# Retention and a gated feed-forward in one kernel: the hand-written order of the lead-in, and of units 4 to 7, rewritten

## The chip, the cores and the metric

The kernel runs on one core of one Trainium2 chip. The metric is the device time of one launch in microseconds. The median of four runs of the kernel before is 298.68 us (298.44 to 298.91).

## The reference

Two layers follow each other. The first is a decayed linear attention (retention) over 8 batches, 8 heads, 576 positions and a head size of 64. The second is a feed-forward of width 2048 over the resulting 4608 tokens of width 512.

```python
scores = scale * np.matmul(q, k.transpose(0, 1, 3, 2))
gamma  = 1.0 - 2.0 ** (-5.0 - np.arange(H))
Dmat   = np.where(rel >= 0, gamma[:, None, None] ** rel[None], 0.0)   # rel = row - column
x = np.matmul(scores * Dmat, v)      # then (B, S, H * D) -> tokens x 512
h = x @ w_in
out = (h * sigmoid(1.702 * h)) @ w_out
```

Because the decay is a power of the distance, the part of the sum that lies in earlier blocks of 64 positions can be carried in a state of 64 x 64 per head; only the block on the diagonal needs scores and a mask.

## The kernel before

**Units and chunks.** The 4608 tokens are cut into 36 units of 128 rows, four units to a chunk, so nine chunks. A unit has two blocks of 64 rows. For each unit the kernel computes x transposed (in xT), and for each chunk the two products of the feed-forward: "up" (x with w_in, 16 steps f of 128 columns, and the Gelu into gT) and "down" (gT with w_out, four units r by four steps s of four matmuls each, then a copy to osb and a store).

**The steps of a unit, with their lines.**
- `load_kq` (L214), `load_v` (L227): DMAs issued by GpSimd (POOL); k and q are cast to bf16 on the way. Twelve slots each. `load_win` (L252) and `load_wout` (L259) bring the weights, each in four parts; they stand in the same queue.
- `transpose_pe` (L344) transposes k or q on TensorE (PE) into a PSUM bank; `transpose_copy` copies it to kqT, on ScalarE (ACT, L354) or VectorE (DVE, L357). `transposes` does both for a unit. From unit 8 on `dma_transpose` (L371) on SyncE's queue (SP) takes their place.
- `scale_v` (L336, DVE) multiplies v with the inverse decay, giving vp.
- `scores` (L477, PE, banks C and D) and `scores_out` (L486, DVE), which applies the mask and writes pm.
- The state. For units 0 to 3, `state_half` (L383 on PE, bank K, and L393 on ACT) accumulates in PSUM and casts after each block. Later, `state_both` (L406, banks K and E) makes both blocks' updates, `state_sum` (L419, L421, DVE) adds them to the running sum in stm, and `state_cast` (L430, ACT) casts the sums of some units to kv.
- `inter` (L461, PE, banks X and Y) multiplies q with the state, `values` (L499, PE) adds masked scores times vp in two halves, and `x_out` (L514) or `x_out_pair` (L524) multiplies with the decay factors gq on DVE and writes xT.

`block1(u)` is inter, values, second state half, values and x_out for one unit. `block(j)` is the same for the pair of units 2j and 2j+1, with the next pair's `ahead` (scores and state_both) between the two halves of values, and the next pair's `ahead_out` (masks, sums, cast) after the x_outs.

**What sets the order.** Nothing but the order in which the program calls these functions: each engine gets its instructions as a list, in that order, and waits on semaphores that are worked out from the names of tiles and banks read and written (`op`, class Program). No scheduler moves anything. An engine therefore stands still when the instruction at its head waits, whatever is behind it. The order is written out by hand in `lead_in` (units 0 to 3 and the up steps of chunk 0, then its down steps with a table `work` that hangs steps of units 4 to 7 on (r, s)), and in `steady` for chunks 1 to 8. `warm` (L649) issues matmuls whose result nobody reads.

**Banks.** A and B take the results of up and down in turn; a bank is free again when ACT has read it (Gelu at L541 or L555, copy to osb at L572). Up is done at full width by `up` (L536) or in groups of two or four steps over one or two units by `up_group` (L550).

**Where the change lies.** In chunk 0 the down steps are called in the order (0,0), (1,0), (0,1), (1,1), (0,2), (1,2), (0,3), (1,3), then (2,0) to (2,3) and (3,0) to (3,3). Before the change, units 4 and 5 are transposed after (0,3) and (1,3), their scores and states come at (2,0), units 6 and 7 are transposed after (2,1) and (2,3), and block(2), with the scores and states of units 6 and 7 inside, stands after (3,0). block(3) stands behind the fourth of chunk 1's sixteen up groups. In chunk 1's down steps, ahead(4) stands after (0,0), block(4) after (1,0), block(5) after (2,2).

Of the kernel before, what the change touches and what calls it, by code (L numbers as in the profile page):

```python
# [13 lines left out]
P = 128  # L14
# [144 lines left out]
def bass_retnet_parallel__then__act_gelu_quick_kernel(  # L159
# [10 lines left out]
    with es:  # L170
# [340 lines left out]
        def x_out(u, slot, hh):  # L511
            ch, j = divmod(u, 4)
            ty = unit_info(u)[2]
            op("dve", lambda e: e.tensor_tensor(  # L514
                xT[ch % 2][:, slice(hh, 4, 2), P * j : P * j + P], xbank(hh, slot),
                gq[:, ty, slice(hh, 4, 2), :], ALU.mult),
               reads=[XB[hh]] + [f"gq{a}_{ty}" for a in range(4)],
               writes=[xkey(u, hh)])
# [67 lines left out]
            scores_out(u, 1, 0)  # L586
            scores_out(u, 1, 1)

        def block1(u):
            started.clear()  # L590
            inter(u, u % 2)
            o = values(u, u % 2, 0)
            if unit_info(u)[1] < 2:
                state_half(u, 1)
            values(u, u % 2, 1, [o])
            x_out(u, u % 2, 0)
            x_out(u, u % 2, 1)

        def ahead(j):
            if 2 * j < NU:  # L600
# [5 lines left out]
        def ahead_out(j, cast=True):  # L606
            if 2 * j >= NU:
                return
            scores_out(2 * j, 2, 0)
            scores_out(2 * j, 2, 1)  # L610
            for u in (2 * j, 2 * j + 1):
                for a in range(2):
                    state_sum(u, a)
            if cast:
                state_cast(2 * j, 2 * j + 2)

# [27 lines left out]
            o = down_out(c, r, b, **kw)  # L644
            last_store[o.dma] = o

        def warm(n):
            for i in range(n):
                op("pe", lambda e: e.matmul(  # L649
                    bank["A"].ap(), gT[1][:, 0, 0:P], gT[1][:, 0, :], skip_group_check=True),  # L650
                   reads=["warm"], writes=["A"])

        def gelu_table():
            op("act", lambda e: e.activation(gT[1][:, 1, 0:4], gT[1][:, 0, 0:4], AF.Gelu_apprx_sigmoid),
# [2 lines left out]
        def lead_in():  # L657
            load_kq0(0)
            load_kq0(1)
            iota_small()  # L660
            iota_large()
            load_v(0)
            load(1)
            load_win(0)
            load(2)
            load_win(1)
            load(3)
            load_win(2)
# [12 lines left out]
            g_powers()  # L681
            gelu_table()
            cast_kq0(0, "dve")
            cast_kq0(1, "dve")
            transpose_pe(0, 0, "E")
            transpose_copy(0, 0, "E", "dve")
            warm(1)
            transpose_pe(0, 1, "B")
            transpose_copy(0, 1, "B", "act")
            warm(4)  # L690
            scores(0)
            scale_v(0)
            gq_next(1)
            scores_out(0, 1, 0)
            scores_out(0, 1, 1)
            state_half(0, 0)
            warm(2)
            transpose_pe(1, 0, "E")
            transpose_copy(1, 0, "E", "act")
            warm(1)  # L700
            transpose_pe(1, 1, "B")
            transpose_copy(1, 1, "B", "act")
            gq_next(2)
            block1(0)
            scale_v(1)
            warm(2)
            scores(1)
            warm(3)
            state_half(1, 0)
            scores_out(1, 1, 0)  # L710
            scores_out(1, 1, 1)
            warm(3)
            block1(1)
            warm(4)
            up_group(0, 0, 2, 0, 2, "A")
            transpose_pe(2, 0, "E")
            transpose_copy(2, 0, "E", "dve")
            up_group(0, 2, 2, 0, 2, "B")
            transpose_pe(2, 1, "E")
            transpose_copy(2, 1, "E", "act")  # L720
            warm(2)
            scale_v(2)
            scores(2)
            state_half(2, 0)
            gq_next(3)
            scores_out(2, 1, 0)
            scores_out(2, 1, 1)
            warm(2)
            up_group(0, 4, 2, 0, 2, "A")
            block1(2)  # L730
            up_group(0, 6, 2, 0, 2, "B")
            transpose_pe(3, 0, "E")
            transpose_copy(3, 0, "E", "dve")
            up_group(0, 0, 4, 2, 3, "A")
            transpose_pe(3, 1, "E")
            transpose_copy(3, 1, "E", "act")
            scale_v(3)
            up_group(0, 4, 4, 2, 3, "B")
            state_half(3, 0)
            scores(3)  # L740
            scores_out(3, 1, 0)
            scores_out(3, 1, 1)
            up_group(0, 8, 2, 0, 2, "A")
            block1(3)
            up_group(0, 10, 2, 0, 2, "B")
            up_group(0, 8, 2, 2, 4, "A")
            up_group(0, 10, 2, 2, 4, "B")
            up_group(0, 0, 4, 3, 4, "A")
            up_group(0, 4, 4, 3, 4, "B")
            gq_next(4)  # L750
            gq_next(5)
            for f in range(12, NF):
                up(0, f)
            def after8():
                ahead(2)
                scores_out(4, 2, 0)
                scores_out(4, 2, 1)

            def after9():
                transposes(6, "B", "B")  # L760
                for u in (4, 5):
                    state_sum(u, 0)
                    state_sum(u, 1)
                scale_v(6)
                scale_v(7)
                state_cast(4, 6)

            work = {
                (0, 3): lambda: (scale_v(4), transposes(4, "E", "E")),
                (1, 3): lambda: (scale_v(5), transposes(5, "C", "C")),  # L770
                (2, 0): after8,
                (2, 1): after9,
                (2, 3): lambda: transposes(7, "C", "C"),
                (3, 0): lambda: block(2, cast=False),
            }
            for r, s in [(i % 2, i // 2) for i in range(8)] + [(i // 4, i % 4) for i in range(8, NF)]:
                down(0, r, s, "AB"[r % 2])
                if (r, s) in work:
                    work[r, s]()
                if s == 3:  # L780
                    finish_unit(0, r, "AB"[r % 2])

        def steady():
            for c in range(1, NCH):
# [10 lines left out]
                if c == 1:  # L795
                    for i in range(16):
                        f0, lo = 2 * (i % 8), 2 * (i // 8)
                        up_group(1, f0, 2, lo, lo + 2, "AB"[i % 2])
                        if i == 1:
                            state_cast(6, 8)  # L800
                        if i == 3:
                            block(3, lambda: None)
                            scale_v(8)
                            scale_v(9)
                        if i == 8:
                            scale_v(10)
                            scale_v(11)
                else:
                    for f in range(NF):
                        up(c, f)  # L810
                        if f % 4 == 0:
                            m = 4 * c + 6 + f // 4
                            if m < NU:
                                scale_v(m)
# [11 lines left out]
                for r in range(4):  # L826
                    for s in range(4):
                        down(c, r, s, "AB"[r % 2])
                        if c == 1 and r == 1 and s == 0:
                            scale_v(12)  # L830
                            scale_v(13)
                        if c == 1 and (r, s) == (0, 0):
                            ahead(4)
                            ahead_out(4)
                        if (r, s) in (((1, 0), (2, 2)) if c == 1 else ((0, 0), (2, 0))):
                            j = 2 * c + 2 + r // 2
                            if 2 * j < NU:
                                block(j, cast=j != 5)
                    finish_unit(c, r, "AB"[r % 2])
                    if c == 1 and r == 3:  # L840
                        state_cast(12, 14)

        lead_in()
        steady()
# [60 lines left out]
```

## Time and profile before

| | us |
|---|---|
| median of four runs | 298.68 |
| the profiled execution's own time | 298.68 |
| its span (first to last instruction) | 296.9 |
| PE busy | 286.4 |
| ACT busy | 135.0 |
| POOL busy | 108.1 |
| DVE busy | 98.7 |

The times are those of one profiled execution. The granted TensorE clock is full over the whole span. A few per cent of the matmul records are missing; a hole of 0.2 us with no reason in a row of matmuls is such a record. A busy share of PE is an upper bound, since matmuls are pipelined and their ends are modelled; start times are what to compare. The chain of waits is read from the last instruction back: at each step it goes to what released the instruction, or to the one before it on its engine. PEld is the weight load of a matmul. "issue" in the chain is time in which an engine waited for nothing that the profile shows.

Landmarks of the PE's start times in the timeline: first up group 13.88, chunk 0's first down step 33.59, chunk 1's up steps 52.80, its down steps 68.00, chunk 2's up steps 85.02, its down steps 99.40.

### The profile page before, as it was taken

Reading aid. Unit: us, or ns where it says so; the run is one execution under the profiler, and the core shown is the slowest. Engines: PE = TensorE matmul, PEld = TensorE weight load, DVE = VectorE, ACT = ScalarE, POOL = GpSimd, SP = SyncE. Lnnn points to the kernel's source line nnn. Section 1 sums busy time; section 2 is a strip of 40 time slices with the busy share of each in tenths; the row PEclk is TensorE's granted clock in tenths of the full one; section 3 lists DMA queues with packets and bytes.
Section 4 is the critical chain, followed back from the end, with each engine's and each line's share of the span. In section 5 each row is a group of like instructions: output and inputs, shape, how many; then the busy total and the mean of one; then the engine's idle time right before and its main releaser. Section 6 shows DMA issues by size and latency. Waiting matters only on the chain.

```text
span 296.9 us, 7882 instructions
## 1 busy us (share of the span) xinstructions
PE 286.4 (96%) x3551; PEld 141.8 (48%) x3583; DVE 98.7 (33%) x198; ACT 135.0 (45%) x236; POOL 108.1 (36%) x137
## 2 busy tenths in 40 slices
PE   8989998999999999999999999999999999999996
PEld 2568455785533454345434543454344434443344
DVE  6555037424661345024701480038005700410000
ACT  8346444573246324642464237523652275216611
POOL 9999488000870760291029401930080000000000
PEclk9999999999999999999999999999999999999999
DMA  9999999979999995599269926991994050110021
GB/s 156 185 208 206 202 221 251 248 127 162 129 233 169 116 202 173 121 167 185 80 138 132 208 69 162 149 201 45 177 92 92 36 144 0 38 73 35 0 73 71
DMA packets 117234, 40.63 MB, mean 137 GB/s; under 512 B 106064, under 2 KB 110416, under 8 KB 117200
## 3 DMA queue, kind: packets, MB, share of 16 engines
q0 software_dynamic: 80160, 22.81, 67.0%
q1 hardware_dynamic: 37040, 17.31, 23.6%
q8 instruction: 28, 0.46, 0.6%
q14 instruction: 6, 0.05, 0.1%
HBM read 36.70 MB, written 9.44 MB: 155 GB/s over the span
## 4 chain that ended last, share of the span: by engine, by line
PE 87%; POOL 4%; DMA 4%; ACT 2%; issue 2%; DVE 1%; POOLq 0%; DVEq 0%
PE psA L562 20%; PE psB L562 20%; PE psA L536 17%; PE psB L536 16%; DMA w_in_sb<-in_moe_w_in_dram 4%; PE psA L550 3%; PE psB L550 3%; POOL kqn L214 2%; PE psX L461 2%; POOL vn L227 1%; PE psC L477 1%; POOL w_in_sb L252 1%; PE psX L499 1%; PE psY L499 1%; PE psK L406 1%
## 5 line engine op out<-in xcount | busy, mean ns | idle before, releaser
L214 POOL DMA_DIRECT2D kqn<-in_k_dram x39 | 35.5, 919 | 111.6 <-DMA kqT<-kqn 108.9
L562 PE MATMUL psA<-w_out_sb,gT 128*128 128x512 bf16 (+1 forms) x287 | 66.6, 373 | 2.8 <-issue 2.4
L562 PE MATMUL psB<-w_out_sb,gT 128*128 128x512 bf16 (+1 forms) x285 | 63.7, 373 | 1.0 <-issue 1.0
L536 PE MATMUL psA<-xT,w_in_sb 128*128 128x512 bf16 x231 | 59.3, 379 | 0.4 <-ACT gT L541 0.4
L536 PE MATMUL psB<-xT,w_in_sb 128*128 128x512 bf16 x225 | 59.2, 379 | 0.4
L524 DVE TENSOR_TENSOR xT<-psX,gq 128x512 bf16<-128x512 f32 x16 | 11.1, 691 | 119.7 <-PE psX L499 119.7
L430 ACT ACTIVATE kv<-stm 128x1024 bf16<-128x1024 f32 (+1 forms) x16 | 15.2, 949 | 68.6 <-DVE stm L421 68.6
L562 PEld LDWEIGHTS psB<-w_out_sb,gT 128*128 128x128 bf16 x288 | 27.8, 98 | 32.6 <-issue 1.2
L562 PEld LDWEIGHTS psA<-w_out_sb,gT 128*128 128x128 bf16 x304 | 27.7, 98 | 31.8 <-ACT gT L541 2.5
L541 ACT ACTIVATE gT<-psA 128x512 bf16<-128x512 f32 x58 | 34.6, 597 | 15.7 <-PE psA L536 15.7
L541 ACT ACTIVATE gT<-psB 128x512 bf16<-128x512 f32 x58 | 34.6, 597 | 15.2 <-PE psB L536 15.2
L227 POOL DMA_DIRECT2D vn<-in_v_dram x40 | 37.4, 941 | 2.3 <-issue 2.2
L214 POOL DMA_DIRECT2D kqn<-in_q_dram x39 | 35.7, 926 | 0.5 <-issue 0.5
L536 PEld LDWEIGHTS psA<-xT,w_in_sb 128*128 128x128 bf16 x232 | 18.5, 97 | 32.0 <-ACT gT L541 16.4
L536 PEld LDWEIGHTS psB<-xT,w_in_sb 128*128 128x128 bf16 x232 | 18.1, 97 | 31.9 <-ACT gT L541 15.5
L336 DVE TENSOR_TENSOR vp<-vn,vfac 128x512 bf16<-128x512 f32 x36 | 23.2, 684 | 23.0 <-DMA vn<-in_v_dram 23.0
L572 ACT ACTIVATE osb<-psB 128x512 f32<-128x512 f32 (+1 forms) x18 | 10.6, 587 | 21.6 <-PE psB L562 21.4
L486 DVE TENSOR_TENSOR pm<-psC,mask 128x512 bf16<-128x512 f32 (+1 forms) x20 | 12.6, 629 | 10.7 <-PE psD L477 10.7
L572 ACT ACTIVATE osb<-psA 128x512 f32<-128x512 f32 x18 | 10.6, 587 | 11.4 <-PE psA L562 11.4
L550 PE MATMUL psA<-xT,w_in_sb 128*128 128x256 bf16 (+1 forms) x128 | 14.6, 259 | 0.4 <-DMA w_in_sb<-in_moe_w_in_dram 0.3
L550 PE MATMUL psB<-xT,w_in_sb 128*128 128x256 bf16 (+1 forms) x128 | 14.6, 259 | 0.0
L486 DVE TENSOR_TENSOR pm<-psD,mask 128x512 bf16<-128x512 f32 (+1 forms) x20 | 12.5, 626 | 0.0
(67 smaller groups left out, 257.1 us busy)
## 6 DMA issues: line engine op xcount, KB each, us to landing
vn<-in_v_dram POOLq DMA_DIRECT2D x32, 256.0 KB, 5.4
out_dram<-osb SPq DMA_DIRECT2D x31, 256.0 KB, 2.2
kqn<-in_k_dram POOLq DMA_DIRECT2D x31, 128.0 KB, 5.0
kqn<-in_q_dram POOLq DMA_DIRECT2D x31, 128.0 KB, 5.3
w_in_sb<-in_moe_w_in_dram POOLq DMA_DIRECT2D x8, 256.0 KB, 8.8
w_out_sb<-in_moe_w_out_dram POOLq DMA_DIRECT2D x4, 512.0 KB, 16.6
out_dram<-osb SPq DMA_DIRECT2D x10, 128.0 KB, 2.6
vn<-in_v_dram POOLq DMA_DIRECT2D x8, 128.0 KB, 5.5
```

What stands on the lines that cost most here:

```text
L214: e.dma_start(kqn[sl][p0 : p0 + n, which, :, :], src[b, :, s0 : s0 + n, :].rearrange("h p d -> p h d"),)
L227: e.dma_start(vn[sl][p0 : p0 + n, :, :], v[b, :, s0 : s0 + n, :].rearrange("h p d -> p h d"))
L336: op(eng, lambda e: e.tensor_tensor(vp[u % NVP].ap(), vn[sl].ap(), vfac[:, ty, :, None].to_broadcast([P, H, DH]), ALU.mult), reads=[f"vn{s ...
L430: op("act", lambda e: e.activation(kv[:, i0 % NKV : i0 % NKV + n, :, :], stm[:, i0 % 8 : i0 % 8 + n, :, :], AF.Copy), reads=[f"stm{(i0 + i ...
L461: op("pe", lambda e, g=g, pb=pb, hh=hh, hp=hp, s=s, a=a, i=prev[a]: e.matmul(xbank(hh, slot)[64 * pb : 64 * pb + 64, g, 64 * a : 64 * a + 64],
L486: op("dve", lambda e: e.tensor_tensor(pm[(u0 // 2) % 2][hh][:, c0:c1].rearrange("p (a i) -> p a i", i=64), ps32(SB[hh])[:, c0:c1].rearrang ...
L524: op("dve", lambda e: e.tensor_tensor(xT[ch % 2][:, slice(hh, 4, 2), P * jj : P * jj + 2 * P].rearrange("p g (u t) -> p u g t", u=2), ps32 ...
L536: op("pe", lambda e, a=a: e.matmul(bank[b][:, n0:n1], w_in_sb[:, a, P * f : P * f + P], xT[c % 2][:, a, n0:n1], start=(a == 0), stop=(a == ...
L541: op("act", lambda e: e.activation(gT[c % 2][:, f, n0:n1], bank[b][:, n0:n1], AF.Gelu_apprx_sigmoid), reads=[b], writes=[f"g{c % 2}_{f}_{j ...
L550: op("pe", lambda e, a=a, f=f, i=i: e.matmul(bank[b][:, n * i : n * i + n], w_in_sb[:, a, P * f : P * f + P], xT[c % 2][:, a, P * lo : P * ...
L562: op("pe", lambda e, f=f: e.matmul(bank[b][:, 0 : n1 - n0], gT[c % 2][:, f, P * r : P * r + P], w_out_sb[:, f, n0:n1], start=(f == 0), sto ...
L572: op("act", lambda e: e.activation(dst, src, AF.Copy), reads=[b], writes=[f"osb{i}_{n0}"])
```

## The change

- `block1` can leave out its x_outs (no call uses it), `warm` can write another bank than A, and `ahead_out` without a cast now calls the state sums ahead of the masks.
- In `lead_in`, unit 0's second transpose copy moves from ACT to DVE, unit 0's and unit 1's scale_v move up, the gq factors move down, and the warm matmuls are distributed anew (32 instead of 31). Units 2 and 3 get their second transpose in bank D; unit 2's block1 moves ahead of the up group of f = 4 and 5, and unit 3's ahead of the group of f = 8 and 9.
- In chunk 0's down steps, the transposes of units 4 and 5 move to (1,3) and (2,0), with one copy on DVE; their scores and states to (2,1), with the sums ahead of the masks; block(2), without the next pair, to (3,1); units 6 and 7 are transposed after (3,2) and (3,3).
- In `steady`, the scores and states of units 6 and 7 stand behind chunk 1's first up group, their cast is split in two behind the third and fourth, and block(3) stands behind the sixth. In chunk 1's down steps ahead(4) stands after (0,2), block(4) after (1,2), block(5) after (3,0). The cast of units 10 and 11 stands alone after (1,3), and that of units 12 and 13 becomes two casts behind f = 1 and f = 3 of chunk 2's up steps.

The core of the diff:

```diff
         def ahead_out(j, cast=True):
...
-            scores_out(2 * j, 2, 0)
-            scores_out(2 * j, 2, 1)
+            if cast:
+                scores_out(2 * j, 2, 0)
+                scores_out(2 * j, 2, 1)
             for u in (2 * j, 2 * j + 1):
                 for a in range(2):
                     state_sum(u, a)
+            if not cast:
+                scores_out(2 * j, 2, 0)
+                scores_out(2 * j, 2, 1)
...
             transpose_pe(0, 1, "B")
-            transpose_copy(0, 1, "B", "act")
-            warm(4)
+            transpose_copy(0, 1, "B", "dve")
+            scale_v(0)
+            warm(2)
             scores(0)
-            scale_v(0)
-            gq_next(1)
             scores_out(0, 1, 0)
             scores_out(0, 1, 1)
+            gq_next(1)
             state_half(0, 0)
-            warm(2)
             transpose_pe(1, 0, "E")
             transpose_copy(1, 0, "E", "act")
-            warm(1)
+            warm(2)
             transpose_pe(1, 1, "B")
             transpose_copy(1, 1, "B", "act")
-            gq_next(2)
+            scale_v(1)
             block1(0)
-            scale_v(1)
-            warm(2)
+            warm(1)
             scores(1)
-            warm(3)
-            state_half(1, 0)
             scores_out(1, 1, 0)
             scores_out(1, 1, 1)
-            warm(3)
+            warm(4)
+            state_half(1, 0)
+            warm(2)
             block1(1)
-            warm(4)
+            warm(5)
             up_group(0, 0, 2, 0, 2, "A")
+            up_group(0, 2, 2, 0, 2, "B")
             transpose_pe(2, 0, "E")
             transpose_copy(2, 0, "E", "dve")
-            up_group(0, 2, 2, 0, 2, "B")
-            transpose_pe(2, 1, "E")
-            transpose_copy(2, 1, "E", "act")
-            warm(2)
+            warm(1, "C")
+            transpose_pe(2, 1, "D")
+            transpose_copy(2, 1, "D", "act")
+            warm(3, "C")
+            scores(2)
             scale_v(2)
-            scores(2)
-            state_half(2, 0)
-            gq_next(3)
             scores_out(2, 1, 0)
             scores_out(2, 1, 1)
+            gq_next(2)
             warm(2)
+            state_half(2, 0)
+            warm(2)
+            block1(2)
+            gq_next(3)
             up_group(0, 4, 2, 0, 2, "A")
-            block1(2)
             up_group(0, 6, 2, 0, 2, "B")
             transpose_pe(3, 0, "E")
             transpose_copy(3, 0, "E", "dve")
+            transpose_pe(3, 1, "D")
+            transpose_copy(3, 1, "D", "act")
+            scale_v(3)
             up_group(0, 0, 4, 2, 3, "A")
-            transpose_pe(3, 1, "E")
-            transpose_copy(3, 1, "E", "act")
-            scale_v(3)
-            up_group(0, 4, 4, 2, 3, "B")
+            scores(3)
             state_half(3, 0)
-            scores(3)
             scores_out(3, 1, 0)
             scores_out(3, 1, 1)
+            up_group(0, 4, 4, 2, 3, "B")
+            block1(3)
             up_group(0, 8, 2, 0, 2, "A")
-            block1(3)
...
-            def after8():
+            def ahead45():
                 ahead(2)
-                scores_out(4, 2, 0)
-                scores_out(4, 2, 1)
-
-            def after9():
-                transposes(6, "B", "B")
                 for u in (4, 5):
                     state_sum(u, 0)
                     state_sum(u, 1)
-                scale_v(6)
-                scale_v(7)
                 state_cast(4, 6)
+                scores_out(4, 2, 0)
+                scores_out(4, 2, 1)
 
             work = {
-                (0, 3): lambda: (scale_v(4), transposes(4, "E", "E")),
-                (1, 3): lambda: (scale_v(5), transposes(5, "C", "C")),
-                (2, 0): after8,
-                (2, 1): after9,
-                (2, 3): lambda: transposes(7, "C", "C"),
-                (3, 0): lambda: block(2, cast=False),
+                (1, 3): lambda: (scale_v(4), transposes(4, "E", "D", "dve")),
+                (2, 0): lambda: (transposes(5, "E", "D", "dve"), scale_v(5)),
+                (2, 1): ahead45,
+                (3, 1): lambda: block(2, lambda: None),
+                (3, 2): lambda: (transposes(6, "C", "D", "dve"), scale_v(6)),
+                (3, 3): lambda: (transposes(7, "E", "K", "dve"), scale_v(7)),
             }
...
                         up_group(1, f0, 2, lo, lo + 2, "AB"[i % 2])
-                        if i == 1:
-                            state_cast(6, 8)
+                        if i == 0:
+                            ahead(3)
+                            ahead_out(3, False)
+                        if i == 2:
+                            state_cast(6, 7)
                         if i == 3:
+                            state_cast(7, 8)
+                        if i == 5:
                             block(3, lambda: None)
...
                         up(c, f)
+                        if c == 2 and f in (1, 3):
+                            state_cast(12 + f // 2, 13 + f // 2)
...
-                        if c == 1 and (r, s) == (0, 0):
+                        if c == 1 and (r, s) == (0, 2):
                             ahead(4)
                             ahead_out(4)
-                        if (r, s) in (((1, 0), (2, 2)) if c == 1 else ((0, 0), (2, 0))):
-                            j = 2 * c + 2 + r // 2
+                        if (r, s) in (((1, 2), (3, 0)) if c == 1 else ((0, 0), (2, 0))):
+                            j = 2 * c + 2 + (r >= 2)
                             if 2 * j < NU:
-                                block(j, cast=j != 5)
+                                block(j, cast=c != 1)
                     finish_unit(c, r, "AB"[r % 2])
-                    if c == 1 and r == 3:
-                        state_cast(12, 14)
+                    if c == 1 and r == 1:
+                        state_cast(10, 12)
```

More of the change, by code (lines that the diff above doesn't have):

```diff
@@ L587, in score1, with block1 @@
             scores_out(u, 1, 1)
-        def block1(u):
+        def block1(u, xo=True):
             started.clear()
@@ L595, in block1 @@
             values(u, u % 2, 1, [o])
-            x_out(u, u % 2, 0)
-            x_out(u, u % 2, 1)
+            if xo:
+                x_out(u, u % 2, 0)
+                x_out(u, u % 2, 1)
         def ahead(j):
@@ L645, in finish_unit, with warm @@
             last_store[o.dma] = o
-        def warm(n):
+        def warm(n, b='A'):
             for i in range(n):
                 op("pe", lambda e: e.matmul(
-                    bank["A"].ap(), gT[1][:, 0, 0:P], gT[1][:, 0, :], skip_group_check=True),
-                   reads=["warm"], writes=["A"])
+                    bank[b].ap(), gT[1][:, 0, 0:P], gT[1][:, 0, :], skip_group_check=True),
+                   reads=["warm"], writes=[b])
         def gelu_table():
```

## Prediction

> **What bounds the kernel now.** I began with the page: the busy time of each engine, then the chain that ended last.
>
> ```profile
> PE 286.4 (96%) x3551; PEld 141.8 (48%) x3583; DVE 98.7 (33%) x198; ACT 135.0 (45%) x236; POOL 108.1 (36%) x137
> q8 instruction: 28, 0.46, 0.6%
> PE 87%; POOL 4%; DMA 4%; ACT 2%; issue 2%; DVE 1%; POOLq 0%; DVEq 0%
> ```
>
> TensorE (PE) carries the chain. The chain starts as loads, becomes PE work once a w_in landing ends, and stays on PE but for a few holes. So a change in the order of the small steps pays only where PE stands still after that landing. The second view is the chain of waits in the lead-in (start, length, what):
>
> ```profile
> 13.41 10.58 DMA w_in_sb<-in_moe_w_in_dram
> 23.98 0.05 issue
> 24.03 1.05 PE psA L550 x8
> ...
> 25.73 0.98 PE psB L550 x8
> ```
>
> Everything ahead of 24.03 is waiting for this load (win2), or hidden by it. Between the two up groups lies unit 3's block1. The third view, the timeline of VectorE there, shows the other gate, the landing of unit 3's v:
>
> ```profile
> 22.08 0.69 DVE L336 TENSOR_TENSOR vp<-vn,vfac 128x512 bf16<-128x512 f32 x1 [0.29 <-DMA vn<-in_v_dram]
> ```
>
> The fourth is the chain over the down steps of chunk 0. Its pieces on ACT, and the "issue", are the holes:
>
> ```profile
> 41.37 0.50 ACT osb L572
> 41.87 0.05 issue
> 41.91 1.04 PE psA L562 x4
> ...
> 47.55 0.98 ACT kqT L354 x2
> 48.53 0.04 issue
> 48.57 0.21 PE psC L477
> ...
> 51.03 0.67 issue
> 51.71 1.25 PE psB L562 x5
> ```
>
> At 41.91 PE waits for the copy out of bank A, which stands on ACT behind unit 4's two transpose copies. At 48.57 the scores of units 6 and 7 wait for unit 7's copies, behind the state cast. At 51.03 PE waits for nothing that the profile names. The last view is the chain at the start of chunk 2's up steps:
>
> ```profile
> 85.22 0.60 ACT osb L572
> 85.82 0.94 ACT kv L430
> 86.76 0.50 ACT gT L541
> 87.26 0.05 issue
> 87.30 1.04 PE psA L536 x4
> ```
>
> One cast of four state tiles (1.05 us) ahead of the first Gelu holds bank A.
>
> [...] q8 has 28 packets in 0.46 MB, 16 KB each, for some 7,170 PE instructions (3,583 weight loads, as many matmuls). [...] I read the 0.67 us hole as a late block, since 256 instructions (128 matmuls) before it PE entered block(2) with 120 matmuls of 64x64 in 1.45 us; the packet ran from 49.24 to 50.26, and the next only from 56.08. [...] loads issued 0.9 us apart land up to 19 us later (landings here and below are the issue in the timeline plus the time to landing in the tile's view), so moving compute doesn't move the landings of the lead-in, whose issues keep their order and wait for nothing. [...] Here 128x512 takes 0.42 us as transpose copy on DVE, 0.59 on ACT, and 0.68 as a mask.
>
> **The change, part by part.** One group of up steps is 0.87 us, a down step of four matmuls 0.863, eight transposes 0.45, a cast of four tiles 1.05, of two 0.63; back to back, ACT's instructions overlap by about 0.1.
>
> *Units 0 to 2, warm matmuls.* Unit 1's chain is shortened: its x_out, now ending at 13.73, ends near 13.0 (v1 lands at 9.57; then one scale, two x_outs of unit 0 and two masks of 0.69 and four times 0.35 to 0.42; block1 and x_out follow). Win0 lands at 13.41, win1 at 18.39, so all of this is hidden: 0. The transpose copies that go to DVE, the gq steps and the 32 instead of 31 warm matmuls lie in the same cover. If it were gone, the gain would be at most 0.7. On DVE unit 1's scale now waits for v1 ahead of unit 0's x_out; behind it stand the masks of unit 1, and PE has its warm matmuls.
>
> *Unit 3's block1 ahead of the group that needs win2.* It waits for v3 instead. Scale ends at 22.77, PE 0.06 later; state_half 0.25, the unit-2 group 0.99 (22.28 to 23.27 in the trace), block1(3) 0.65 (25.01 to 25.66), up 8 0.86: 22.83 + 0.25 + 0.99 + 0.65 + 0.86 = 25.58 against 25.66. **-0.08**: what goes is the win2 wait, and the wait for v3 is late next.
>
> *Transposes of units 4, 5 after (1,3) and (2,0).* The copy of bank A is now issued ahead of unit 4's, and bank A is wanted only after down (1,3) and the transposes. That hole (41.40 to 41.91) goes: **-0.50**. Unit 5's transposes, in banks E and D, wait for unit 4's copies: DVE about 41.3, ACT 41.7; PE is there at 41.7. No wait, 0.6 if ACT is late by one instruction.
>
> *State sums ahead of masks.* ahead45 ends near 43.7; four sums of 0.46 give the cast 45.8 to 46.9, masks end at 47.0. block(2) stands four down steps later, at 47.4. Nothing waits; with the masks first, the cast would end at 48.2.
>
> *block(2) without ahead(3), which moves into chunk 1's up groups.* The wait at 48.57 goes: 1.45 measured against 1.24 for the undisturbed block of units 12 and 13 (100.26 to 101.50): **-0.21**. But two short bursts cost more than one: block(3) alone takes 1.01 with its drain between the halves, so block(2) some 0.94, and ahead(2) took 0.78; together 1.72 against 1.24: **+0.47** (bounds +0.25 and +0.6). Unit 6's and 7's copies move to DVE and ACT after (3,2) and (3,3), long after their landings (the last, v7, at 46.8); v7's scale ends near 51.9, as the scores of ahead(3) finish.
>
> *The hole at 51.03.* Over the same 128 matmuls PE now has two down steps, sixteen transposes and an up group between the bursts: 4.6 us in place of 3.2. The block came 3.9 us after PE entered (47.8 to 51.71). **-0.67**; ends 0 and -0.67.
>
> *State casts in halves.* (6,7) and (7,8) behind chunk 1's groups 2 and 3: gelu, cast, gelu, cast fit into the 0.27 us of slack of each group, with block(3) two groups later as cover: 0. block(5) in chunk 1 found its cast late (PE pieces of 0.17 at 79.57): the cast of units 10, 11 now stands behind (1,3), five steps before: **-0.16**. The cast of units 12, 13 becomes two of 0.63 behind f = 1 and 3. Chunk 2's up steps take 14.38 now (85.02 to 99.40), chunk 3's, without a cast, 13.82. With the overlap each half fits: **-0.56**; if they don't overlap, 0.33 stays.
>
> *ahead(4), block(4), block(5) later.* Their transposes by DMA start when v13 has landed (63.55), whatever PE does, and land at 66.47, 67.82, 69.18, 70.53, 73.74, 74.74. Down steps of chunk 1 would now start near 66.8 instead of 67.78 (68.00 less one missing record of 0.22); ahead(4) comes three steps later, at 69.4. In its old place it would stand at 67.7, just ahead of the 67.82. Cost 0. SP's queue holds the same stores and transposes, POOL's the same loads; those of units 14 up hang on the transpose that lands at 74.74, not on PE. They are due after 98, landed by 95.6 to 98.1.
>
> Sum: -0.08 - 0.50 - 0.21 + 0.47 - 0.67 - 0.16 - 0.56 = **-1.71 us**. The profiled execution took 298.68 with a span of 296.9, and 298.68 is also the median of the four runs. So 296.97: **297.0 us**, span 295.2. A change of 0.2% (0.6 us) is about what a measurement of this kernel can tell from none.
>
> **The rivals.**
> - *The refill is late again* (same size): bursts are still there, and the packet waits among the loads. For: the next block needed 4.4 us to start. Against: 1.4 us more between bursts. 297.7.
> - *The landings take the gain back:* DMA transposes a little later than now make ahead(4) wait at 69.4. For: they hang on v13 alone. Against: 1.6 us of room. If all won so far is lost, only -0.3 of the later casts stays: 298.4.
> - *Slower:* one mechanism, the refill requested as block(2) begins (47.5). If it takes as long as the following one did (51.7 to about 58.6, 6.9 us), ahead(3), which reaches the block's end 4.6 us on, stands 2.3 us, and that eats the whole gain: 297.0 + 2.3 = 299.3. It decides from 4.6 us up; the sign turns at 6.3. For: the same queue, in the same crowded stretch. Against: the packet of this very request took 3.9.
> - *It doesn't do what it says:* the lead-in's order is hidden by win0, win1, and v3; that is already counted, with -0.08 for all of it.
>
> **How the numbers follow.** Forecast 0.60, late refill 0.19, landings 0.09, slower 0.08, other 0.04 (a further gain). The forecast's own range is 296.5 to 297.5 (split cost and casts at their ends). With 297.7 inside and half of the landings' case, 296.4 to 298.1 holds 8 in 10. Faster by over 0.6: 0.60 + 0.19 + 0.04 - 0.02 for spread = 0.81; within: 0.10; slower: 0.09.
>
> **What would show it.** block1(3) ahead of the win2 group, whose first matmul starts near 24.7; no ACT piece in the chain from 39 to 48; down steps of chunk 1 from 66.8; chunk 2's up steps in 13.9 us; no "issue" of over 0.3 on PE. Wrong if PE shows such an "issue" between 47 and 60, if scores wait for a kqT by DMA, or if up 8 starts after 25.

## The result, and the profile after

| | before | after |
|---|---|---|
| median, us (lowest to highest) | 298.5 (297.37 to 301.99), 63 runs | 297.9 (297.02 to 299.52), 44 runs |
| time over the time before | 1 | 0.9983, interval 0.9974 to 0.9992 |
| span of the profiled execution | 296.9 | 296.1 |
| that execution's own time | 298.68 | 297.88 |

The change gains 0.6 us of the median, 0.17% with 0.08 to 0.26 as the interval. The forecast was 1.71. The page of after, with the busy time of each engine and the shares of the chain:

```profile
PE 285.5 (96%) x3553; PEld 141.7 (48%) x3584; DVE 100.5 (34%) x203; ACT 133.1 (45%) x233; POOL 108.2 (37%) x137
PE 94%; issue 2%; DMA 2%; POOL 1%; DVE 1%; ACT 0%; POOLq 0%
```

In the chain, ACT has gone from 2% to 0%: the waits for copies and casts that the prediction listed are gone. "issue" has not shrunk. To see where the time went I cut the span at the landmarks (start times of PE; a start that has a missing record just ahead of it is moved back by 0.22). The column on the right is an experiment, after with some loads held back, told below.

| stretch of the span, us | before | after | change | after, loads held |
|---|---|---|---|---|
| start to first down step of chunk 0 | 33.59 | 33.02 | -0.57 | 34.31 |
| to first down step of chunk 1 | 34.19 | 34.69 | **+0.50** | 33.27 |
| to chunk 2's up steps | 17.24 | 16.97 | -0.27 | 16.98 |
| those up steps | 14.38 | 13.96 | -0.42 | 13.95 |
| from there to the end | 197.45 | 197.42 | -0.03 | 197.25 |

The second row was to be shorter by 0.91 (the terms -0.50, -0.21, +0.47 and -0.67), and it is longer by 0.50. The first row is the place of the lead-in; it varies between executions, and an experiment below prices it. The chain of after through the second row (start, length, what):

```profile
41.63 0.22 PE psD L344 x4
41.85 0.86 PE psA L562 x4
...
51.88 1.05 issue
52.93 0.21 PE psK L406
...
59.84 0.11 issue
59.95 0.94 PE psB L550 x7
```

Where before had an ACT copy of 0.50 at 41.37, PE goes from unit 4's transposes straight to bank A: that hole is gone, and so is the wait for unit 7's copies. But at 51.88, in the state updates of units 6 and 7, PE stands for 1.05 us on "issue", longer than the 0.67 that was to go. The waits of after from 47 to 62 show that the weight loads stand as well, for nothing that the profile can name (us in total, times, longest):

```profile
PEld psK L406 <- issue: 1.2, 1, 1.2
PE psK L406 <- issue: 1.1, 1, 1.1
```

Both halves of PE stop in the middle of a row of equal instructions whose operands are all there: VectorE had written the last of them, unit 7's scaled v, by 51.32. From the last start before the hole to the first after it is 1.24 us. In the packet records of the instruction queue one 16 KB block runs from 50.46 to 51.43; PE resumes 1.50 after its end. Before it was 49.24 to 50.26 and 51.71, so 1.45 after.

At the start of chunk 2's up steps, in the chain of after, the ACT pieces of before (osb, the cast of 0.94, the Gelu) are gone:

```profile
82.90 1.94 PE psB L562 x9
84.84 0.86 PE psA L536 x4
85.71 0.86 PE psB L536 x4
```

In before the first Gelu began 1.64 us after the start of its matmuls (86.66 and 85.02), behind the cast that ACT had begun at 85.71; in after, with no cast ahead of it, 1.06 (85.74 and 84.68).

### The profile page after: what moved, and what is told of

It reads as the page before. It is cut to its first block, busy times and chain, and to the rows that moved or that the text cites. A ratio compares the mean times of both kernels' runs of the same rounds, so it can differ in the third digit from the quotient of the medians.

```text
span 296.1 us, 7890 instructions
## 1 busy us (share of the span) xinstructions
PE 285.5 (96%) x3553; PEld 141.7 (48%) x3584; DVE 100.5 (34%) x203; ACT 133.1 (45%) x233; POOL 108.2 (37%) x137
## 4 chain that ended last, share of the span: by engine, by line
PE 94%; issue 2%; DMA 2%; POOL 1%; DVE 1%; ACT 0%; POOLq 0%
PE psA L562 21%; PE psB L562 20%; PE psA L536 17%; PE psB L536 17%; PE psB L550 4%; PE psA L550 4%; PE psX L461 2%; DMA kqn<-in_q_dram 2%; PE psC L477 1%; PE psY L499 1%; PE psA L654 1%; PE psX L499 1%; PE psK L406 1%; PE psD L477 1%; PE psE L406 1%
```

## The experiments

**Theory.** The hole at 51.88 is a block of PE instructions that comes late. I take a block as 256 of them, 128 matmuls with their weight loads: an estimate from the 28 packets of 16 KB and the 3584 weight loads in the trace of after, and from the distances between the stops in experiments 1 and 2. The loads that are on their way at that time (some 14 us from issue to landing) hold its packet back, and PE comes to the end of the block ahead of it before it is there. The times of a packet below are counted from PE's entry into the block ahead, 128 weight loads before the packet's own. With the block ends that experiments 1 and 2 give, 45 of the 56 packets in the traces of before and after start 0.05 to 4.69 us after that point, nine 0.05 to 1.24 us before it, and the last of each trace 3.03 and 4.33 us before. So they mostly follow it, but what asks for a packet isn't shown. **Rivals.** It is a real wait that the new order makes (a bank, a copy, a landing), and would stay with the instructions it belongs to; or the gain was lost elsewhere, in the lead-in or by casts and blocks that are no better where they stand now. Ratios are to the kernel before, timed on the same chip, with a 95% interval.

| kernel | ratio | interval | span | first down step to end |
|---|---|---|---|---|
| after | 0.9983 | 0.9974 to 0.9992 | 296.1 | 263.04 |
| after, 36 more PE instruction pairs | 1.0058 | 1.0037 to 1.0079 | 299.4 | 266.07 |
| before, 36 more PE instruction pairs | 1.012 | 1.0078 to 1.0162 | 300.4 | 266.37 |
| after, ahead(3) one group later | 1.0004 | 0.9981 to 1.0027 | 297.2 | 262.92 |
| after, loads held | 0.996 | 0.9939 to 0.998 | 295.8 | 261.45 |
| before, loads held | 0.9986 | 0.9966 to 1.0007 | 295.4 | 262.12 |
| before, with the new lead-in | 1.0002 | 0.9984 to 1.0021 | 295.8 | 263.13 |
| before, with the later casts and blocks | 0.998 | 0.9967 to 0.9993 | 295.3 | 261.99 |
| before, with the new units 4 to 7 | 1.0008 | 0.9992 to 1.0024 | 296.3 | 263.53 |
| after, loads held, ahead(3) back in block(2) | 0.9983 | 0.9964 to 1.0002 | 296.5 | 262.65 |
| after, loads held, 36 more PE pairs | 1.0047 | 1.0026 to 1.0069 | 297.6 | 263.51 |

Before has 263.26 in the last column. Each span, and each number of the last column, is from one profiled execution.

**1 and 2. Shifting the blocks.** If the hole lies at the end of a block, it moves when instructions are added far ahead of it, and nothing else changes. Two of the warm matmuls are replaced by 38 small ones, in after and in before (there four become two). The matmuls' results are read by nobody.

```diff
+        def pad(n):
+            for i in range(n):
+                b, r, c = "CD"[i % 2], 64 * (i % 2), 64 * (i // 2 % 2)
+                op("pe", lambda e, b=b, r=r, c=c: e.matmul(
+                    bank[b][c : c + 64, 0:64], gT[1][r : r + 64, 0, 0:64], gT[1][r : r + 64, 0, 0:64],
+                    skip_group_check=True), reads=["warm"], writes=[b])
...
             block1(1)
-            warm(5)
+            warm(3)
+            pad(38)
             up_group(0, 0, 2, 0, 2, "A")
```

> The kernel after, with two of the five warm matmuls ahead of the first up group replaced by 38 tiny ones of 64x64 (about the same 0.4 us on TensorE, hidden by the landing of w_in; nothing reads them). This moves every later TensorE instruction 36 matmuls (72 instructions) further within its 256-instruction block. Theory 1, a late refill of instructions: the hole of 1.05 us in the state updates of units 6 and 7 sits at the end of a block; that end now falls into the scores of units 6 and 7 and the one before it into the states of units 4 and 5, some 8 us apart instead of 5, so the hole goes and the time falls by 1.0 to 1.4 us against the kernel after (about 296.7, ratio to the kernel before 0.994). Theory 2, a wait for data or a bank in that step: the hole stays at the same instruction (L406) and the time stays at 0.998 of before.

> The kernel before, with two of the four warm matmuls ahead of the first up group replaced by 38 tiny ones of 64x64, hidden by the landing of w_in. Theory 1: the block's end leaves the down steps of unit 3 and falls into the states of units 6 and 7 inside block(2), 5.7 us after the end before it instead of 3.2; the hole of 0.67 us at 51.03 shrinks to 0 to 0.3 or moves into block(2), time 0.3 to 0.7 us below before (ratio 0.998 to 0.999). Theory 2: a hole of 0.67 us stays between the down steps (3,2) and (3,3), ratio 1.000.

Measured: the ratios 1.0058 and 1.012. In the chain of after with the pad, the state updates of units 6 and 7 run through, and a hole stands in block(3):

```profile
52.28 0.01 PE psE L406 x2
52.29 0.98 PE psB L550 x8
...
57.32 0.51 issue
57.82 0.21 PE psX L499
```

So the wait doesn't belong to the state updates. It belongs to a number. Counted over all weight loads in the trace, PE stops ahead of number 730 in after; with the pad, ahead of 350 (0.44 us at 22.19, in unit 3's state), 858 and 1881, the last in the place told below; in before ahead of 731, in before with the pad ahead of 731, 859 and 1882. All are 89 to 94 more than a multiple of 128, whatever work stands there. (Of matmuls some records are missing, 3553 of 3584 are there in after; of weight loads all are.) Counted in instructions, with two for each matmul and one for each semaphore instruction that the trace has among the weight loads, the agreement is closer: the number of instructions ahead of each stop is 193 or 194 modulo 256. The same holds for every "issue" of over 0.4 us on PE after its first up group, 13 in the twelve traces. In before the pad likewise takes the hole from 51.03, and holes stand at 49.71 (1.00) and 58.17 (0.74). The part of the expectation that failed is the time: both kernels are slower, since the ends of all later blocks move too, and one falls behind block(8) in chunk 3, where I had not looked. The holes account for most of it: after with the pad has 0.44, 0.51 and 2.25 us where after has 1.05 and 0.11, so 2.04 more, and the medians are 2.38 apart (300.28 and 297.9). The ratio of before with the pad comes from 6 executions. The chain of after with the pad there:

```profile
129.24 0.14 PE psX L461
...
130.44 2.25 issue
132.69 3.99 PE psA L562 x11
136.68 1.53 PE psB L562 x6
```

Some 120 matmuls of 64x64 pass in 1.20 us. PE enters the block ahead at 129.17; the packet starts at 129.57, takes 1.45, and the first weight load follows 1.43 after its end. The packet started only 0.40 us after PE's entry. The block ahead was used up in 1.06 us, and the shortest time from PE's entry into it to the first weight load after a stop that these traces show is 2.60 (experiment 10). In before with the pad the same place shows 2.01 us.

**3. Moving the state updates.** ahead(3) goes behind the second up group of chunk 1, and the two casts behind the fourth and fifth.

```diff
-                        if i == 0:
+                        if i == 1:
                             ahead(3)
                             ahead_out(3, False)
-                        if i == 2:
-                            state_cast(6, 7)
                         if i == 3:
+                            state_cast(6, 7)
+                        if i == 4:
                             state_cast(7, 8)
```

> The kernel after, with the scores and states of units 6 and 7 behind chunk 1's second up group instead of the first, and their two casts one group later; block(3) stays. Theory 1: TensorE reaches the block's end 0.87 us later, the refill comes when it came, so the hole of 1.05 us shrinks to about 0.2; time 0.6 to 0.9 us below after (ratio to before 0.995 to 0.996). Theory 2: the hole moves along with the step and keeps its 1.05 us, ratio 0.998.

Measured: 1.0004. The hole in the state updates is gone, but this chain has new waits in its place:

```profile
52.40 0.50 ACT osb L572
...
52.94 1.05 PE psB L550 x8
...
58.12 0.53 ACT kv L430
...
58.69 0.21 PE psX L461
...
60.71 0.50 issue
```

PE now wants bank B before its copy, which stands behind unit 7's copy on ACT; block(3) waits for its cast, and the next block end has a hole of 0.50. What the move wins it loses at these three places, and the 0.6 to 0.9 us that were expected didn't come. It doesn't tell the theory from a rival by its time, only by the hole's place.

**4. Holding loads back.** In after, POOL issues the loads of units 8 to 11 early, and they take some 14 us from issue to landing. They are now issued only when unit 4's keys have been transposed.

```diff
-            for u in range(4, NPE + 4):
+            for u in range(4, NPE):
                 load(u)
...
-                (2, 0): lambda: (transposes(5, "E", "D", "dve"), scale_v(5)),
+                (2, 0): lambda: (transposes(5, "E", "D", "dve"), scale_v(5),
+                                 [load(u, after=["T4_0"]) for u in range(NPE, NPE + 4)]),
```

> The kernel after, with the loads of units 8 to 11 issued only once unit 4's keys are transposed (near 41 us) instead of from about 29 us on, so that fewer packets stand in the DMA queues when the refill is asked for near 47 us. Theory 1 with the queue as the cause of the delay: the refill's packet starts within 1.5 us in place of 3.5, the hole shrinks to under 0.3 us, time 0.8 to 1.2 below after if the last load still lands by 64 (ratio 0.994 to 0.995). Theory 2: the hole stays, 0.998. If the loads land later than 66, the scores of units 8 and 9 wait for their transposes by DMA and the time rises by as much as they are late beyond 67.

Measured: 0.996, 296.92 us; the interval lies below 1 and is the lowest of the study, though it overlaps that of after by a little (0.9974 to 0.998). The chain at the place of the hole:

```profile
51.77 0.87 PE psA L550 x8
...
53.33 0.01 PE psE L406 x2
53.34 0.98 PE psB L550 x8
```

No "issue": scores and state updates run through. PE passes number 730 without a stop. It is 128 ahead of it at 48.19, and the packet runs from 49.30 to 50.38, so it starts 1.10 us after that; in after the two are 46.90 and 50.46, 3.56 us. The DMA view from 42 to 51 shows what differs (KB each, median us from issue to landing), first in after:

```profile
vn<-in_v_dram POOLq DMA_DIRECT2D x4, 256.0 KB, 14.3
...
kqn<-in_q_dram POOLq DMA_DIRECT2D x3, 128.0 KB, 14.5
```

and then in after with loads held:

```profile
vn<-in_v_dram POOLq DMA_DIRECT2D x2, 256.0 KB, 5.8
...
kqn<-in_q_dram POOLq DMA_DIRECT2D x2, 128.0 KB, 5.9
```

The engines move nearly as much in both (246 and 227 GB/s), but a load that is issued there takes 14 us to land in the one and 6 in the other. Between these two kernels the packet's delay goes with how long a load takes to land more than with how much the engines move. The row of the stage table that had failed is now 33.27 us, 0.92 below before, where the prediction had 0.91.

**5. The same in before.** The edit is that of 4, with the held loads after unit 4's transposes at (0, 3).

```diff
-            for u in range(4, NPE + 4):
+            for u in range(4, NPE):
...
-                (0, 3): lambda: (scale_v(4), transposes(4, "E", "E")),
+                (0, 3): lambda: (scale_v(4), transposes(4, "E", "E"),
+                                 [load(u, after=["T4_0"]) for u in range(NPE, NPE + 4)]),
```

> The kernel before with the loads of units 8 to 11 held until unit 4's keys are transposed, and nothing else. Theory that the depth of the DMA queues delays the refill: the packet of the block that ends near 51 starts within 1.5 us of the block's beginning, the hole of 0.67 goes, ratio 0.9975 to 0.998. Rival, that the loads' time of landing is what a_loads_held gained by: the hole stays, ratio 1.000 or, if the loads of units 8 and 9 come later, above.

Measured: 0.9986, with 1 inside the interval, so the time alone shows no gain. In its chain the hole of 0.67 is gone, and twelve matmuls follow each other with no gap, while the wait for unit 7's copies is still there:

```profile
47.25 0.98 ACT kqT L354 x2
...
48.27 0.21 PE psC L477
...
49.12 2.70 PE psB L562 x12
```

The packet of that block starts 0.34 us after PE has entered the block ahead (47.52 and 47.19), where before had 1.76. So my reading of the hole of before was right. It was the inference from it to after that failed. With no late block on either side, the second row is 33.35 here and 33.27 in 4: there the new order of units 4 to 7 gains 0.08, where -0.50, -0.21 and +0.47 had promised 0.24.

**6 to 8. The three parts alone.** Before with the diff's part in `lead_in` up to chunk 0's up steps; before with the later casts and blocks of chunks 1 and 2; before with the table `work` and chunk 1's up groups. All three have the new `ahead_out` too, which puts block(2)'s state sums ahead of its masks on DVE. Their cores:

```diff
             transpose_pe(0, 1, "B")
-            transpose_copy(0, 1, "B", "act")
-            warm(4)
-            scores(0)
+            transpose_copy(0, 1, "B", "dve")
             scale_v(0)
...
+            up_group(0, 4, 4, 2, 3, "B")
             block1(3)
+            up_group(0, 8, 2, 0, 2, "A")
```

> The kernel before with the change's lead-in alone (units 0 to 3 and the warm matmuls). Theory: all of it is hidden by the landings of w_in and v3, so the time stays (0 to -0.1 us, ratio 0.9995 to 1.000), and the hole of about 0.67 us in the down steps near 51 stays, since the count of matmuls ahead of it changes by one. Rival: the 0.57 us by which the first down step came earlier in the profile after is the work of the lead-in's edits and not of earlier landings; ratio 0.998.

```diff
+                        if c == 2 and f in (1, 3):
+                            state_cast(12 + f // 2, 13 + f // 2)
...
-                        if c == 1 and (r, s) == (0, 0):
+                        if c == 1 and (r, s) == (0, 2):
...
-                    if c == 1 and r == 3:
-                        state_cast(12, 14)
+                    if c == 1 and r == 1:
+                        state_cast(10, 12)
```

> The kernel before with the change's order of chunk 1's down steps and the casts of chunk 2 alone (ahead(4) after (0,2), block(4) after (1,2), block(5) after (3,0), casts of units 12 and 13 apart, sums ahead of masks without a cast). Theory: the wait of block(5) and the wait for the Gelu in chunk 2 go, -0.6 to -0.75 us, ratio 0.9975 to 0.998; the hole near 51 stays. Rival: these waits are covered or another takes their place, ratio 1.000.

```diff
-                (3, 0): lambda: block(2, cast=False),
+                (3, 1): lambda: block(2, lambda: None),
+                (3, 2): lambda: (transposes(6, "C", "D", "dve"), scale_v(6)),
+                (3, 3): lambda: (transposes(7, "E", "K", "dve"), scale_v(7)),
...
+                        if i == 0:
+                            ahead(3)
+                            ahead_out(3, False)
```

> The kernel before with the change's order of units 4 to 7 alone (the table of down steps of chunk 0, the first up groups of chunk 1). Theory of the late refill: the waits for the copy of bank A and for unit 7's copies go (-0.7), the split of block(2) and ahead(3) costs 0.47, the hole of 0.67 goes, and one of 1.0 to 1.3 comes in the states of units 6 and 7 and one of 0.1 to 0.3 near 60: together 0 to +0.6 us, ratio 1.000 to 1.002. Rival, that the hole in the kernel after comes from the lead-in or the steady part: no hole here, -0.9 us, ratio 0.997.

Measured: 1.0002, 0.998 and 1.0008. The lead-in is worth nothing that can be measured, and with it alone the hole of before stays, 0.66 us at 49.84, ahead of weight load 732. First down steps start at 32.77 to 33.59 in the four profiles with the old lead-in and no pad, and at 32.62 to 34.31 in the five with the new one. The 0.57 of the stage table is no gain of the change. The casts and blocks alone gain 0.6 us, all that after gains. Units 4 to 7 alone gain nothing, and their chain has the hole of after:

```profile
51.62 0.89 issue
52.51 0.19 PE psK L406
...
59.42 0.11 issue
59.53 0.92 PE psB L550 x7
```

Another thing shows in the kernel with the casts alone: the hole of before is 0.13 in its profile (at 50.78) and not 0.67, though nothing ahead of it on PE is changed. Its packet was at 48.42 to 49.30. The size of such a hole is thus not fixed by PE's order alone.

**9. One burst again.** Held loads, and ahead(3) back inside block(2), with units 6 and 7 transposed after (2, 3) and (3, 0). This takes the +0.47 of the split away.

```diff
-                (3, 1): lambda: block(2, lambda: None),
-                (3, 2): lambda: (transposes(6, "C", "D", "dve"), scale_v(6)),
-                (3, 3): lambda: (transposes(7, "E", "K", "dve"), scale_v(7)),
+                (2, 3): lambda: (transposes(6, "E", "K", "dve"), scale_v(6)),
+                (3, 0): lambda: (transposes(7, "C", "D", "dve"), scale_v(7)),
+                (3, 1): lambda: block(2, cast=False),
...
-                        if i == 0:
-                            ahead(3)
-                            ahead_out(3, False)
```

> The kernel after with the loads of units 8 to 11 held, and besides with units 6 and 7 transposed after (2,3) and (3,0), their scores and states back inside block(2) after (3,1), their cast whole behind chunk 1's second up group and block(3) behind the fourth, as in the kernel before. Theory, that the separate burst costs 0.47 us and the refill is in time once the queues are short: 0.3 to 0.5 us below a_loads_held, ratio to the kernel before 0.994 to 0.995. Rival, that one burst of 120 matmuls again runs ahead of its refill: a hole of 0.3 to 0.7 us in the last down steps, ratio 0.996 to 0.998.

Measured: 0.9983, above 4 by 0.0023, with intervals that overlap. Its chain:

```profile
48.93 0.14 PE psX L461
...
50.09 1.40 issue
51.48 1.89 PE psB L562 x8
```

The joined burst takes 1.16 us, and behind it PE stands 1.40. PE is 128 ahead of the stop at 47.69; the packet starts 1.30 later (48.98 to 50.12) and PE resumes 1.37 after it, 3.80 in all, where PE had 2.33 us of work. With the burst whole in one block, a packet that starts about as soon as in 4 (1.30 and 1.10 us) still comes too late.

**10. Held loads with the pad.** The edits of 1 and 4 together.

```diff
-            for u in range(4, NPE + 4):
+            for u in range(4, NPE):
...
-            warm(5)
+            warm(3)
+            pad(38)
```

> The kernel with the held loads, and with the 38 tiny matmuls of a_pad36. If holes come where the end of a 256-instruction block meets loads in the queues: the hole near 57.8 in block(3) (0.5 us in a_pad36) goes, since fewer loads are queued there, while those at 22.6 in unit 3's state (0.44 us) and after block(8) near 132.7 (2.25 us), where the loads are as before, stay; about 299, ratio 1.001 to 1.005. Rival, that a_pad36's hole of 2.25 us was an accident of that one profiled execution: no hole near 132, ratio 0.995 to 0.996 as for the held loads alone.

Measured: 1.0047. The hole of 0.51 at 57.32 is gone: its packet starts 3.06 us after PE has entered the block ahead, in place of 3.87, and a load issued between 50 and 57 lands after some 7 us in place of 13. But the hole of 0.44 at 22.19, which was to stay since no load is held there, is gone too, so one profile of each can't show that holding the loads alone did it. Behind block(8) 1.34 us at 131.08 stay, where no held load has a part: PE enters the block ahead at 129.81, the packet runs from 129.87 to 130.95, and PE goes on 1.46 after its end, 2.60 in all for 1.06 us of work. That hole is of another kind than those that went in 4 and 5. There the packet started 3.56 and 1.76 us after PE's entry, and 1.10 and 0.34 with the loads held; here it starts after 0.06, and the burst is over before the block is there.

## Why the prediction was wrong

- **The step that failed is "The hole at 51.03 ... -0.67".** It took the 3.9 us that the block had needed before (4.2 by the count of weight loads) as what it needs, and the 4.6 us of work between the bursts as cover. The cover was sized well: PE had 4.76. The need is no constant: in after the block was usable 6.03 us after PE had entered the one ahead, 3.56 for the packet to start, 0.97 for the packet, 1.50 to resume. So a hole came back in ahead(3), 1.24 from start to start, with 0.11 at the next block's end, in place of a gain of 0.67. This is close to the rival "The refill is late again", with a size that it had not foreseen, and to the case of the slower one, short of its 6.9 us. With loads held, from the first down step to the end, 263.26 falls to 261.45: 1.81, where the forecast without its lead-in term had 1.63. The ratio 0.996 says 1.2, with 0.6 to 1.8 as the interval.
- The lead-in, -0.08: nothing (1.0002). Up 8 stood behind block1(3), at 24.28 against the 24.7 named. That it is all hidden was right.
- The copy of bank A, -0.50, and unit 7's copies, -0.21: both waits are out of the chain of after. The split of block(2) and ahead(3), +0.47 (1.72 less 1.24 is 0.48): not measured by itself, since joining them brought a hole of 1.40. For the three together the held pair of kernels shows -0.08 in place of -0.24, from one profile each.
- block(5), -0.16: the stretch of chunk 1's down steps is 0.27 shorter, in after, with held loads and in the kernel of the casts alone. Casts of units 12 and 13, -0.56: -0.42; what stays is 0.14, between no overlap (0.33) and a full one. Together -0.69 for -0.72.
- "The landings take the gain back": no run shows it. The down steps of chunk 1 run without a wait for a transpose by DMA.
- The text named what would make it wrong, an "issue" between 47 and 60 on PE, and that is what happened (1.05 us at 51.88). The longest hole at the end of a block in these runs is 2.25 us.

What stays open: why the packet of after starts 3.56 us after PE's entry and not 1.76 (47.49 to 49.24) as before, when the landing times of the loads are nearly the same in both (13.4 and 14.3 us). It goes with the order of units 4 to 7 and not with the moment at which PE enters the block ahead. In the six kernels with neither held loads nor the pad PE enters that block 13.9 us after the first down step. With the old order (before, and before with the new lead-in or the later casts) the packet starts 1.18 to 1.76 us after that; with the new one (after, ahead(3) one group later, and before with the new units 4 to 7) 3.42 to 3.56. The stores of the first two units are issued earlier in the new order, 6.9 and 8.7 us after the first down step in place of 8.3 and 9.8; whether they hold the packet back no run shows. Nor could I say beforehand how large such a hole is in a given execution.

## What to carry to other kernels

When PE's trace shows an "issue" hole in a row of ready instructions, look at the packets of the instruction queue and count where its blocks end; a change that moves instructions moves these ends, and an old hole that goes may come back in a new place (here 0.67 us at 51.03, then 1.05 at 51.88). Keep short bursts of tiny matmuls away from them (the hole of 2.25 us stands behind some 120 that pass in 1.20 us), or hold back loads that aren't due (here the packet then started after 1.10 us and not 3.56). A gain of half a microsecond in one stage should be priced with the block ends of every later stage, and measured part by part.

## What the runs showed of the hardware

- From the end of an instruction packet to the first weight load of its block passed 1.21 to 1.52 us wherever PE stood waiting for it for over 0.4 us (1.45 before, 1.50 after, eleven more in the experiments). It comes on top of the packet's own 0.96 to 1.45 us, and lies in the same bounds with loads held (1.37 and 1.46).
- After the 2.25 us hole at 130.44, the granted clock was 1.00 up to 133.6, 0.50 from there to 137.0, and 1.00 again. The down steps' matmuls were 0.43 us apart in that stretch instead of 0.216, so the 11 of the chain shown took 3.99 us. After the hole of 2.01 us in before with the pad, and the 1.34 of experiment 10, the clock stayed at 1.00. One case isn't enough to say what sets it. It adds some 1.6 us to the profiled execution (11 times 0.216 is 2.38), and so to the 266.07 of the table, but not to the median: 17 of the 22 executions of that kernel have a mean clock of 1.00.
- 36 more PE instruction pairs ahead of the first up group, with the first down step at 33.32 and 34.02, inside the 32.62 to 34.31 of the kernels without them, made after slower by 0.75% (1.0058 over 0.9983) and before by 1.2%.
